# Summing keys and values over eight neighbours: three additions of halves in place of one strided tensor_reduce

## The chip, the cores and the metric

The kernel runs on one core of a Trainium2 chip. A core has five engines with instruction queues of their own, each executed in order: TensorE (PE in the profile; its weight loads are shown apart, as PEld), VectorE (DVE), ScalarE (ACT), GpSimd (POOL) and SyncE (SP), which here issues DMAs. They share the on-chip memory SBUF; TensorE writes its results to a second one, PSUM. Semaphores make an instruction on one engine wait for instructions on another. The metric is the time of one execution on the device, in microseconds (us); less is better.

## The reference

Attention with pooled keys and values, and behind it a layer of a transformer's feed-forward network:

```python
def _attn_ref(q, k, v):                       # 8 batches, 8 heads, 576 positions, 64 wide
    k_p = k.reshape(B, H, Sp, 8, D).mean(axis=3)      # 72 pooled keys: means of 8 neighbours
    v_p = v.reshape(B, H, Sp, 8, D).mean(axis=3)
    scores = scale * np.matmul(q, k_p.transpose(0, 1, 3, 2))
    ...                                       # softmax over the 72 keys
    return np.matmul(attn, v_p)
def _moe_ref(x, w_in, w_out):                 # 4608 tokens, 512 -> 2048 -> 512
    h = x @ w_in
    g = h * (1.0 / (1.0 + np.exp(-1.702 * h)))
    return g @ w_out
```

What the change touches is the sum over eight neighbours in the first two lines of the attention.

## The kernel before

The kernel works through the eight batches one after the other, and interleaves the attention of one batch with the feed-forward products of the batch before it, so that TensorE always has matmuls of one of the two. The order of all work on all engines is written out by hand in one long table (`ORDER`, a string of names such as `V:red1_0#0`, with V for VectorE, G for GpSimd, A for ScalarE, P for TensorE and D for a DMA); the program's code only says what each named task consists of and which buffers it reads and writes. So an engine never chooses: if the next task of its queue has to wait, all that stands behind it on that engine waits too.

For each batch b and each group u of four heads, keys and values of the first 512 positions are loaded into one SBUF tile `kv` (128 partitions, 2 x 512 numbers of fp32 in each). A partition holds, for each of two head pairs, eight neighbours of 64 numbers one behind the other. `spread` sums the eight neighbours into `red` (128 x 128), and then writes `red` into the block-diagonal tiles `kbd` (keys) or `vbd` (values) that TensorE multiplies with (a TENSOR_TENSOR on line 918). There are 32 such sums, four in each batch. Three of batch 0 are done by TensorE (line 886). The other 29 are done by VectorE with one `tensor_reduce` each: line 893 for five of batches 0 and 1 (named in `SUMMED`), where `red` is a PSUM buffer, and line 908 for the 24 of batches 2 to 7, where `red` lies in SBUF. The eight neighbours stand 64 numbers apart, so the reduce reads its 1024 numbers with a stride of 256 bytes.

The `kv` tile has a single buffer: the load of the next keys or values (SyncE, lines 797 and 811) waits until the sum has read the last ones. The PSUM buffers of `red` in batch 1 come from the same ring of two as those of the scores (`sps`, line 1126) and of attention times values (`pav`, lines 1365 to 1376).

Other names that are spoken of below: `stage` (lines 1762, 1790) and `xt`, `xs` (line 1457) are sums of weights and of inputs on VectorE or GpSimd, which the feed-forward products need; `ha` and `hb` (line 1880) are those products in PSUM; `shared` (line 1902) is VectorE's addition of an `hb`, which frees it for TensorE; `glall` (line 1934) and `gl` (line 1705) are differences that GpSimd or VectorE forms from two SBUF tiles; `w` and `raw` (lines 1641, 1627) are GpSimd's share in splitting the weights; `x` (line 1416) is VectorE's addition from a `pav`, which frees it; `vt` (line 1067) is a copy from SBUF to SBUF; `sc` and `tail` (lines 1198, 1232) belong to the softmax.

Of the kernel before, what the change touches and what calls it, by code (L numbers as in the profile page):

```python
# [14 lines left out]
ALU = mybir.AluOpType  # L15
AX = mybir.AxisListType
# [3 lines left out]
POOL = 8  # L20
# [553 lines left out]
def attention_moe_kernel(ctx: ExitStack, tc: tile.TileContext, q, k, v, w_in, w_out, out):  # L574


    nc = tc.nc
    B, H, S, D = q.shape
# [45 lines left out]
    def buf(pool, shape, dtype, tag, name, bufs=None, fifo=False):  # L624
        n = bufs or {"xpool": 2, "moe": 2, "ps_o": 4, "ps_h": 2, "ps_a": 2}.get(pool.name, 1)
        ring = rings.setdefault((pool.name, tag), Ring(n, fifo, pool.name))
        kw = {"bufs": bufs} if bufs else {}
        return Buf(ring, lambda: pool.tile(shape, dtype, tag=tag, name=name, **kw), name)
# [15 lines left out]
    def dve(n, emit, reads, writes, rate=1.0, due=None, also=(), port=False):  # L644
        return plan.add("DVE", 0.07 + n / 960.0 * rate, emit, reads, writes, due, also=also, port=port)
# [6 lines left out]
    def pe(ns, emit, reads, writes, due=None, also=(), mode="f32"):  # L652
        return plan.add("PE", ns * 1e-3, emit, reads, writes, due, also=also, mode=mode)
# [7 lines left out]
        out=mask4[0:96], in_=ident[0:96].rearrange("p (r h e) -> p h r e", r=4, h=4), axis=AX.XY, op=ALU.add  # L661
# [3 lines left out]
        out=mask4[96:128, 0:2],  # L665
        in_=ident[96:128].rearrange("p (r a e) -> p a r e", r=8, a=2),
        axis=AX.XY,
        op=ALU.add,
# [6 lines left out]
        out=mask, in_=ident.rearrange("p (r h e) -> p h r e", r=4, h=4), axis=AX.XY, op=ALU.add  # L675
# [3 lines left out]
        out=member, in_=ident.rearrange("p (r g e) -> p g r e", r=2, g=POOL), axis=AX.XY, op=ALU.add  # L679
# [92 lines left out]
    class Part:  # L772
# [8 lines left out]
        @property  # L781
        def ref(self):
            return (self.of, self.key)
# [91 lines left out]

    def spread(b, raw, bd, u, nm):

        if b < TURNED:
            red = buf(ps_h if b == 0 else ps_a, [P, 512], F32, "h" if b == 0 else "a", f"red{b}_{nm}")

            def summed():
                return red()[:, 0 : NP * D].rearrange("p (i d) -> p i d", i=NP)

            def windows():
                for w in range(POOL):
                    nc.tensor.matmul(
                        summed(), lhsT=ident, rhs=raw()[:, :, w * D : (w + 1) * D], start=w == 0, stop=w == POOL - 1
                    )

            if (b, nm) in SUMMED:  # L890
                dve(
                    1024,
                    lambda: nc.vector.tensor_reduce(
                        out=summed(), in_=raw().rearrange("p i (w d) -> p i d w", w=POOL), axis=AX.X, op=ALU.add
                    ),
                    [ref(raw)],
                    [red],
                    rate=1.75,
                    also=[bd],
                )  # L900
            else:
                pe(2 * POOL * 111, windows, [ref(raw)], [red], also=[bd])
        else:
            red = buf(att, [P, NP, D], F32, "red", f"red{b}_{nm}")
            summed = red
            dve(
                1024,
                lambda: nc.vector.tensor_reduce(
                    out=red(), in_=raw().rearrange("p i (w d) -> p i d w", w=POOL), axis=AX.X, op=ALU.add
                ),  # L910
                [ref(raw)],
                [red],
                rate=1.75,
                also=[bd],
            )
        dve(
            256,
            lambda: nc.vector.tensor_tensor(
                out=bd()[:, NP * u : NP * (u + 1)],
                in0=summed().unsqueeze(2).broadcast_to([P, NP, 2, D]),  # L920
                in1=mask2i.unsqueeze(1).unsqueeze(3).broadcast_to([P, NP, 2, D]),
                op=ALU.mult,
            ),
            [red],
            [(bd, u)],
            port=b >= TURNED,
        )
# [4 lines left out]
    def sum_keys(b, m):  # L932
# [6 lines left out]
        for u in range(NU):  # L939
            raw = m.k[u] if m.k else fetch_main(b, u, k)  # L940
            if b >= TURNED:
                tl = fetch_tail(b, u)
            spread(b, raw, m.kbd, u, f"k{u}")
            if b < TURNED and u == 0:
                tps = buf(ps_o if b == 0 else ps_a, [P, 512], F32, "o" if b == 0 else "a", f"tps{b}")
# [98 lines left out]
    def sum_values(b, m):  # L1044
        m.vbd = buf(att, [P, NJ, 2, D], F32, "bd", f"vbd{b}", fifo=True)
        for u in range(NU):
            raw = m.v[u] if m.v else fetch_main(b, u, v)
            spread(b, raw, m.vbd, u, f"v{u}")
# [1488 lines left out]
```

## Time and profile before

| | |
|---|---|
| time, median of 3 runs | 877.8 us (876.97, 877.8, 877.99) |
| span of the profiled execution, first to last instruction | 876.5 us |
| TensorE busy | 867.8 us, 99% |
| VectorE busy | 712.3 us, 81% |
| ScalarE busy | 529.5 us, 60% |
| GpSimd busy | 318.0 us, 36% |
| VectorE's reduces of lines 893 and 908 | 29 of some 2.0 us each |
| granted TensorE clock, mean | 1.00 |

The profiled execution is not one of the three timed runs; its span is 1.3 us under their median, and what lies before the first and after the last instruction is not in it. A page of the profile gives for each group of instructions its busy time and the idle time of its engine just before it with what ended it. The timeline gives single instructions with their start and length; one that waits inside the engine is simply longer than its like.

### The profile page before, as it was taken

The numbers are of one execution on the slowest core, as the hardware profiler recorded it, in microseconds if no ns is written. First come the engines' busy times: TensorE is split into PE (matmuls) and PEld (weight loads), VectorE is DVE, ScalarE is ACT, GpSimd is POOL, SyncE is SP. The second block draws the span as 40 slices with busy tenths as digits, with TensorE's granted clock in tenths as the row PEclk, the third lists the DMA queues.
The fourth block names the chain that finished last, engine by engine and source line by source line (L and its number), as shares of the span: only waits on it lengthen the run. The fifth ranks groups of instructions, "written<-read, shape, count | busy, mean of one in ns | idle before, by whom it ended". The sixth has DMA issues, their size and how long they took to land.

```text
span 876.5 us, 15636 instructions
## 1 busy us (share of the span) xinstructions
PE 867.8 (99%) x5322; PEld 775.8 (89%) x5322; DVE 712.3 (81%) x1413; ACT 529.5 (60%) x1170; POOL 318.0 (36%) x325
## 2 busy tenths in 40 slices
PE   8999999999999999999999999999999999999998
PEld 7889888888898999998999999999999988889998
DVE  6999988897879896788887877788878866778887
ACT  4987855547565774767566755677476743455430
POOL 2778753554321113222522242324522123432321
PEclk9999999999999999999999999999999999999999
DMA  9966444576577666756785777667766457978003
GB/s 275 377 219 185 131 133 162 167 228 199 173 226 218 213 209 211 232 159 209 239 245 160 219 215 231 191 200 213 213 200 194 155 182 217 332 230 298 1 13 85
DMA packets 146351, 174.31 MB, mean 199 GB/s; under 512 B 85216, under 2 KB 97504, under 8 KB 146272
## 3 DMA queue, kind: packets, MB, share of 16 engines
q1 hardware_dynamic: 141808, 165.32, 61.1%
q10 hardware_dynamic: 4464, 8.00, 2.5%
q8 instruction: 42, 0.69, 0.3%
q14 instruction: 37, 0.30, 0.1%
HBM read 141.95 MB, written 31.33 MB: 198 GB/s over the span
## 4 chain that ended last, share of the span: by engine, by line
PE 92%; SPq 2%; DVE 2%; DMA 2%; ACT 1%; issue 0%; POOL 0%; POOLq 0%; DVEq 0%; ACTq 0%
PE ha L1880 13%; PE hb L1880 10%; PE m L2386 9%; PE o L2086 8%; PE o L2087 8%; PE o L2088 8%; PE la L2155 5%; PE sps L1126 4%; PE h L1677 3%; PE h L1675 3%; PE h L1676 3%; PE o L1717 3%; PE o L1718 3%; PE o L1719 3%; PE lc L2155 2%; PE lb L2155 1%
## 5 line engine op out<-in xcount | busy, mean ns | idle before, releaser
L1934 POOL TENSOR_TENSOR glall<-shared,ghall 128x256 fp32r<-128x256 f32 x78 | 61.6, 795 | 200.2 <-ACT shared L1927 137.7
L2086 PE MATMUL o<-w,ghall 128*128 128x512 f32 x320 | 127.1, 397 | 0.0
L2087 PE MATMUL o<-w,ghall 128*128 128x512 f32 x320 | 126.2, 394 | 0.0
L2088 PE MATMUL o<-w,glall 128*128 128x512 f32 x320 | 124.9, 390 | 0.0
L2088 PEld LDWEIGHTS o<-w,glall 128*128 128x128 f32 x320 | 60.1, 188 | 13.8 <-DVE glall L1934 0.2
L1880 PE MATMUL ha<-xs,ws 128*128 128x256 f32 x480 | 70.9, 283 | 0.0
L1934 POOL TENSOR_TENSOR glall<-gall,ghall 128x256 fp32r<-128x256 f32 x43 | 33.4, 782 | 102.4 <-ACT gall L1927 73.1
L1880 PEld LDWEIGHTS ha<-xs,ws 128*128 128x128 f32 x480 | 66.2, 190 | 4.4 <-ACT gall L1895 0.2
L1880 PE MATMUL hb<-x,ws 128*128 128x256 f32 x480 | 67.1, 283 | 0.0
L2086 PEld LDWEIGHTS o<-w,ghall 128*128 128x128 f32 x320 | 60.6, 189 | 6.4
L2087 PEld LDWEIGHTS o<-w,ghall 128*128 128x128 f32 x320 | 60.6, 190 | 5.8
L1880 PEld LDWEIGHTS hb<-x,ws 128*128 128x128 f32 x480 | 63.3, 190 | 2.4
L1919 ACT ACTIVATE ghall<-shared 128x256 fp32r<-128x256 f32 x108 | 43.8, 416 | 34.8 <-DVE shared L1902 15.7
L1675 PE MATMUL h<-x,w 128*128 128x512 f32 (+1 forms) x160 | 57.5, 359 | 0.0
L1705 POOL TENSOR_TENSOR gl<-g,gh 128x512 fp32r<-128x512 f32 x27 | 36.6, 1354 | 57.3 <-ACT gh L1697 49.0
L1676 PE MATMUL h<-x,w 128*128 128x512 f32 (+1 forms) x160 | 55.5, 347 | 0.0
L1677 PE MATMUL h<-x,w 128*128 128x512 f32 (+1 forms) x160 | 55.5, 347 | 0.0
L1241 ACT COPY main<-sc 32x256 f32<-32x256 f32 (+2 forms) x109 | 48.6, 446 | 4.9 <-DVE sc L1198 2.5
L1902 DVE TENSOR_TENSOR shared<-shared,hb 128x256 f32<-128x256 f32 x81 | 33.4, 413 | 22.2 <-PE hb L1880 18.5
L1895 ACT COPY shared<-ha 128x256 f32<-128x256 f32 x63 | 23.3, 369 | 42.4 <-PE ha L1880 42.1
L1126 PE MATMUL sps<-k,qt 128*128 128x144 f32 x320 | 45.9, 287 | 0.0
L1717 PE MATMUL o<-w,gh 128*128 128x512 f32 x112 | 45.4, 405 | 0.0
(270 smaller groups left out, 2430.6 us busy)
## 6 DMA issues: line engine op xcount, KB each, us to landing
ws<-wd SPq DMA_DIRECT2D x144, 512.0 KB
shared<-wd SPq DMA_DIRECT2D x48, 256.0 KB
wd<-stage SPq DMA_DIRECT2D x16, 512.0 KB
raw<-in_moe_w_in_dram SPq DMA_DIRECT2D x15, 512.0 KB
raw<-in_moe_w_out_dram SPq DMA_DIRECT2D x15, 512.0 KB
kv_False<-in_k_dram SPq DMA_DIRECT2D x28, 256.0 KB
kv_True<-in_v_dram SPq DMA_DIRECT2D x28, 256.0 KB
out_dram<-osb ACTq DMA_DIRECT2D x28, 256.0 KB
```

What stands on the lines that cost most here:

```text
L1126: nc.tensor.matmul(ps()[:, t * PW : (t + 1) * PW], lhsT=qt()[:, s0 : s0 + P], rhs=m.k2()[:, jj], start=True, stop=True,)
L1675: nc.tensor.matmul(o, lhsT=w[:, 0, j], rhs=xs[:, 0], start=j == 0, stop=False)
L1676: nc.tensor.matmul(o, lhsT=w[:, 1, j], rhs=xs[:, 0], start=False, stop=False)
L1677: nc.tensor.matmul(o, lhsT=w[:, 0, j], rhs=xs[:, 1], start=False, stop=j == NJ - 1)
L1717: nc.tensor.matmul(o, lhsT=gh()[:, i, tok], rhs=w[:, 0], start=f == 0, stop=False)
L1880: nc.tensor.matmul(o, lhsT=wv()[:, r, jj], rhs=xo(k, jj), start=start and n == 0, stop=n == len(terms) - 1,  skip_group_check=not start,)
L1934: engine.tensor_tensor(out=gl(), in0=part(i), in1=gh().bitcast(F32), op=ALU.subtract)
L2086: nc.tensor.matmul(o(), lhsT=gh()[:, tok], rhs=w()[:, 0], start=start, stop=False)
L2087: nc.tensor.matmul(o(), lhsT=gh()[:, tok], rhs=w()[:, 1], start=False, stop=False)
L2088: nc.tensor.matmul(o(), lhsT=gl()[:, tok], rhs=w()[:, 0], start=False, stop=stop)
L2155: nc.tensor.matmul(bank(), lhsT=wv()[:, r, jj], rhs=xs[jj]()[:, k], start=start and n == 0, stop=n == len(terms) - 1, skip_group_check=not ...
L2386: nc.tensor.matmul(banks[i]()[:, i], lhsT=av(r)[:, i * P : (i + 1) * P], rhs=tv(k), start=p == 0 and n == 0 and (i == 0 or banks[0] is not ...
```

## The change

Each of VectorE's 29 reduces becomes three additions. The first adds the upper four neighbours to the lower four (2 x 256 numbers in each partition), in place in the `kv` tile. The second adds the upper two of these to the lower two (2 x 128), in place again. The third adds the last two and writes `red` (2 x 64). Each reads what the one before it wrote. Both inputs of each are in SBUF. The task has the same name, the same place in the order and the same dependences for the rest of the program; the order of the instructions on TensorE, ScalarE, GpSimd and SyncE is the same as before, and on VectorE three instructions stand wherever one stood.

```diff
     def spread(b, raw, bd, u, nm):
 
+        def tree(out):
+            r = raw()
+            for n in (4 * D, 2 * D, D):
+                to = r[:, :, 0:n] if n > D else out()
+                nc.vector.tensor_tensor(out=to, in0=r[:, :, 0:n], in1=r[:, :, n : 2 * n], op=ALU.add)
+
         if b < TURNED:
...
                 dve(
                     1024,
-                    lambda: nc.vector.tensor_reduce(
-                        out=summed(), in_=raw().rearrange("p i (w d) -> p i d w", w=POOL), axis=AX.X, op=ALU.add
-                    ),
+                    lambda: tree(summed),
...
             dve(
                 1024,
-                lambda: nc.vector.tensor_reduce(
-                    out=red(), in_=raw().rearrange("p i (w d) -> p i d w", w=POOL), axis=AX.X, op=ALU.add
-                ),
+                lambda: tree(red),
```

## Rows read from the trace of the kernel before

**Rows 1.** The page: the span, and busy time, share and instructions of each engine
```profile
span 876.5 us, 15636 instructions
PE 867.8 (99%) x5322; PEld 775.8 (89%) x5322; DVE 712.3 (81%) x1413; ACT 529.5 (60%) x1170; POOL 318.0 (36%) x325
```

**Rows 2.** TensorE's longest wait behind VectorE: us in total, times, longest us
```profile
PE pav L1365 <- DVE xt L1425: 0.7, 1, 0.7
```

**Rows 3.** Line 908, the reduces of keys: ns least/median/most, first and last start us
```profile
L908 DVE TENSOR_REDUCE red_k<-kv_False x12: 1928/2016/2072, 115.6 to 609.7; 128x128 f32<-128x1024 f32 x12
```

**Rows 4.** VectorE's additions and multiplications of 512, 256 and 128, from their lines
```profile
L1457 DVE TENSOR_TENSOR xt<-xt x3: 679/681/685, 236.0 to 424.8; 128x512 f32<-128x512 f32 x3
L2332 DVE TENSOR_TENSOR ou<-store x25: 408/419/427, 787.5 to 858.0; 128x256 f32<-128x256 f32 x25
L1198 DVE TENSOR_TENSOR tail<-sc,sps x2: 280/314/347, 24.2 to 44.2; 128x128 f32<-128x128 f32 x1, 128x192 f32<-128x192 f32 x1
```

**Rows 5.** Timeline at 527.5, VectorE and GpSimd: start us, length us, engine, line
```profile
527.53 0.87 DVE L1070 TENSOR_TENSOR vt<-tbd,vt 32x512 fp32r<-32x512 f32 x1
527.82 1.19 POOL L1934 TENSOR_TENSOR glall<-shared,ghall 128x256 fp32r<-128x256 f32 x1
528.43 0.85 DVE L918 TENSOR_TENSOR kbd<-red_k,mask2i 128x256 f32<-128x256 f32 x1
```

**Rows 6.** Timeline at 807.7, GpSimd behind four instructions of VectorE, the last shown
```profile
807.65 2.64 POOL L2332 TENSOR_TENSOR ou<-store 128x256 f32<-128x256 f32 x1 [10.21 <-DVE oc L2326]
...
809.01 0.69 DVE L2326 TENSOR_TENSOR oc<-ou,oc 128x512 fp32r<-128x512 f32 x1
```

**Rows 7.** Timeline at 80.1 to 84.4, values of batch 1
```profile
80.12 1.33 POOL L1641 TENSOR_TENSOR w<-raw,w 128x512 fp32r<-128x512 f32 x1 [0.48 <-ACT w L1634]
...
80.30 2.10 DVE L893 TENSOR_REDUCE red_v<-kv_True 128x128 f32<-128x1024 f32 x1 [0.45 <-DMA kv_True<-in_v_dram]
...
81.41 1.30 POOL L1705 TENSOR_TENSOR gl<-g,gh 128x512 fp32r<-128x512 f32 x1
...
82.67 1.04 POOL L1627 TENSOR_TENSOR raw<-raw 128x512 uint32<-128x512 uint32 x1
...
83.09 0.42 DVE L918 TENSOR_TENSOR vbd<-red_v,mask2i 128x256 f32<-128x256 f32 x1
...
84.39 0.65 PE L1126 MATMUL sps<-k,qt 128*128 128x144 f32 x4
```

**Rows 8.** Timeline at 130.6 to 139.1, keys of batch 2
```profile
130.56 0.76 POOL L1641 TENSOR_TENSOR w<-raws,w 128x256 fp32r<-128x256 f32 x1
130.57 2.02 DVE L908 TENSOR_REDUCE red_k<-kv_False 128x128 f32<-128x1024 f32 x1
...
131.26 3.08 POOL L1762 TENSOR_TENSOR stage<-w 128x512 f32<-128x512 f32 x2
...
138.24 0.42 DVE L1416 TENSOR_TENSOR x<-pav,x 128x256 fp32r<-128x256 f32 x1
...
139.06 0.39 PE L1365 MATMUL pav<-ah,vh 128*128 128x320 f32 x1
```

**Rows 9.** Timeline at 426.0 to 430.2, keys of batch 5
```profile
426.01 1.48 POOL L1457 TENSOR_TENSOR xt<-xt,xt 128x512 f32<-128x512 f32 x1
...
426.37 2.06 DVE L908 TENSOR_REDUCE red_k<-kv_False 128x128 f32<-128x1024 f32 x1
427.45 0.74 POOL L1934 TENSOR_TENSOR glall<-shared,ghall 128x256 fp32r<-128x256 f32 x1
...
428.16 1.29 POOL L1457 TENSOR_TENSOR xs<-xt,xs 128x512 fp32r<-128x512 f32 x1
428.35 1.38 DVE L1067 CAST vt<-tbd 96x512 fp32r<-96x512 f32 x1
...
429.65 0.40 DVE L1902 TENSOR_TENSOR shared<-shared,hb 128x256 f32<-128x256 f32 x1
...
430.24 0.64 PE L1880 MATMUL hb<-x,ws 128*128 128x256 f32 x4
```

## The prediction

> **What bounds the kernel now.** I read the page first: TensorE is busy for 867.8 of 876.5 us [rows 1], so all other engines together can be charged with no more than 8.7 us of its idle time. I then read the list of its waits. Behind VectorE there is one wait to speak of there, a single one of 0.7 us [rows 2]. VectorE is busy for 712.3 us [rows 1], and its reduces take 2.02 us each in the middle [rows 3], 58 us for the 29. A reader should see that these 58 us are almost wholly beside TensorE's work: making VectorE faster takes little off the end, since TensorE has next to nothing left to wait for. The reverse doesn't hold. A result of VectorE that comes too late stops TensorE at once, and a TensorE that is always busy can't make the stop good later. So the question is not only whether three additions are shorter than a reduce, but whether any of the 29 ends later, and by more than TensorE's reserve at that place.
>
> **The change part by part.** Removed: 29 x 2.02 = 58.6 us of VectorE [rows 3]. Added: 29 times an addition of 512, one of 256 and one of 128 numbers per partition. With nothing in the way these take 0.68, 0.42 and 0.28 us [rows 4], and a dependent instruction starts some 0.03 us after the one before it (528.43 against 527.53 + 0.87, [rows 5]): 1.44 us. So alone the tree is 0.58 us shorter, 16.8 us over the 29.
>
> The Trainium skill speaks against even this: "VectorE: DVE Perf Modes", section "The perf-mode tier table (the rule you actually need)", has tensor_reduce and fp32 tensor_tensor both at one element a cycle. By it an estimate for the reduce is 1024 / 0.96 GHz and a fixed part, some 1.2 us, and the tree would be the longer one by about 0.2 us. The measured reduce of 2.02 us disagrees with that page, and the measurement decides.
>
> What the reduce doesn't do, and the additions do, is to compete with GpSimd. The reduces stay between 1.93 and 2.07 us [rows 3], though GpSimd works in most of them. Instructions of VectorE with two inputs in SBUF are different. At 528.43 a `kbd` of 256 numbers takes 0.85 us in place of 0.42, and GpSimd's `glall`, itself held back by `vt`, ends at 529.01 [rows 5]. Three things are read from this. VectorE's instruction is held until about 0.13 us before GpSimd's ends (529.28 - 0.42 = 528.86, against 529.01). GpSimd's is held while VectorE's runs (1.19 us, against 0.74 for its like in [rows 9]). And a gap of 0.03 us between two instructions of VectorE is enough for a waiting GpSimd to go in between. A tree has two such gaps, so with GpSimd busy it can be held three times: before each addition, by up to one instruction of GpSimd, 0.74 to 1.30 us [rows 7, 9].
>
> The skill's "SBUF — State Buffer", section "SBUF: two separate sides", states the same as a rule: the port pair that the two engines share goes whole to whichever starts first, for its entire instruction, against an instruction of VectorE with two SBUF inputs. By that rule too the reduce, with one input, is free of it, and the tree is not; the rows agree.
>
> Where GpSimd rests, the tree ends 0.58 us earlier, and that is worth nothing but at the wait of 0.7 us [rows 2]: 0 to 0.7 us. I take 0, since a gain there needs a tree shortly before it that nothing else on VectorE waits behind, and keep 0.7 as the bound. Where GpSimd is busy I follow the rows, GpSimd's instructions in their order, with the rule above. Of the 29 places I price the three where the delay is largest beside the reserve. TensorE's reserve is the time from the end of the VectorE instruction that releases its matmul to that matmul's start.
>
> At 80.30 [rows 7], the values of batch 1: `w` runs on GpSimd since 80.12 and ends at 81.45, so the first addition begins at about 81.32 and ends at 82.00. `gl` goes in between and ends at 83.17; the second addition runs from 83.04 to 83.46; `raw` goes next, to 84.4, and the third ends at some 84.6, where the reduce ended at 82.40. That is 2.2 us late. Behind it in VectorE's queue stand two instructions on weights and `vbd`, which frees the PSUM buffer that the scores at 84.39 are written to. `vbd` ended at 83.51, a reserve of 0.88. TensorE loses 2.2 - 0.9 = 1.3 us. If the tree starts before `w`, which needs only 0.2 us (the reduce had itself waited 0.45 for its load), the first addition and not `w` goes first, and by the same steps the tree ends about 0.9 late: no loss.
>
> At 130.57 [rows 8], keys of batch 2: `w` of 0.76 started 0.01 us earlier. First addition 131.19 to 131.87; the first `stage`, of about 1.3 like `gl` [rows 7], to 133.05; second addition to 133.34; the second `stage` to 134.5; third addition to 134.7, where the reduce ended at 132.59: 2.1 late. VectorE is then busy without a break worth the name up to `x`, which ends at 138.66 and frees a `pav` for TensorE at 139.06: reserve 0.4, and 0.2 more for short gaps on the way. Loss 1.5. With the tree ahead of `w` by a hundredth, it is 0.9 late, and the loss 0.3.
>
> At 426.37 [rows 9], keys of batch 5: `xt` runs until 427.49. First addition 427.36 to 428.04; `glall` to 428.65; second addition to 428.94; `xs` to 430.1; third addition to 430.25, where the reduce ended at 428.43: 1.8 late. `vt` behind it was itself held by `xs`, some 1.0 of its 1.38 us, so it ends 430.7 at best, and 1.3 later if the next `xt` goes ahead of it. `shared`, which ended at 430.05, ends 1.0 to 2.0 later; it frees the `hb` that TensorE starts at 430.24, reserve 0.2. Loss 0.8 to 1.8; I take 1.4, the middle being 1.3 and the later order the one that the rule gives more often.
>
> Sum: 1.3 + 1.5 + 1.4 = 4.2 us. I take it for the whole, since the errors on its two sides are alike: with the lucky order in the first two places it falls to 0 + 0.3 + 0.8 = 1.1; and there are four more places where GpSimd is busy and the reserve is under the delay, each worth 0.2 to 0.6 by the same steps, which I leave as the upper side, some 1.5 more. The gain of 0.7 at most stands against that. GpSimd loses up to 0.7 us at each held instruction, but it is busy for only 36% [rows 1] and mostly ahead of its readers; I cost this at nothing, and at 1 to 3 us if that reserve fails. SyncE's next load of `kv` waits for the third addition in place of the reduce; the one load that was late at all is the one at 80.30.
>
> **The rivals.** *VectorE keeps its turn between the three additions*, and GpSimd waits for all of them. For it: at 807.65 a GpSimd addition of 0.74 takes 2.64 us, while additions of VectorE go past it, the last of which runs from 809.01 to 809.70 [rows 6]. Against it: those follow each other without a gap and don't read one another's results, where the steps of a tree do, and a dependent start leaves a gap. Then a tree is held once only: at 80.30 it ends 0.4 late, at 130.57 not at all (131.19 + 1.44 = 132.63), at 426.37 0.4 late with 0.2 of reserve. The loss is 0.2, the gain 0 to 0.7: 877.6 us, not slower. This decides if the gap between dependent additions is no longer an opening for GpSimd.
>
> *The delays spread*: all seven places lose, GpSimd's own delays reach TensorE through `glall` and `stage`, and late trees meet new work of GpSimd. Price: 4.2 + 0.3 for the worse order at 426, + 1.5 for the four places, + 2 for GpSimd: 8 us, 885.8. For it speaks that VectorE is 81% busy [rows 1], so delays take long to be worked off; against it that GpSimd is idle for 64%.
>
> *Faster*: 16.8 us less of VectorE reach the end after all. TensorE's idle time behind VectorE, 0.7 us [rows 2], caps that at 877.1, which is no measurable difference; more than that needs a mechanism that I don't see in the rows, such as matmuls slowed unseen by VectorE's reads.
>
> **How the numbers follow.** The profiled execution spans 876.5 us, 1.3 us under the median of 877.8 shown; the loss is added to the median: 877.8 + 4.2 = 882.0. Chances: the forecast 0.54 (878.9 to 884.5), delays that spread 0.14 (885.8), VectorE keeps its turn or the orders fall luckily 0.27 (877.6), faster 0.05. The range reaches from a little under the case that is not slower to the one that spreads, 877.2 to 886.0. A measurement of this kernel can tell some 0.2%, 1.76 us, from no change: below 876.0 is faster, above 879.6 slower. Faster 0.05; same 0.27; slower 0.68 (the little of the forecast that lies under 879.6 is set against the upper end of the lucky orders).
>
> **What would show it.** On VectorE the 29 reduces are replaced by 87 additions of least lengths 0.68, 0.42 and 0.28 us; where GpSimd is at work, by longer ones, whose excess is GpSimd's remainder less 0.13. VectorE's busy time should fall by far less than 17 us, and may rise. GpSimd's `glall`, `gl` and `stage` near trees are longer. TensorE's list of waits has new entries behind VectorE at 84, 139 and 430 us (scores behind `vbd`, `pav` behind `x`, `hb` behind `shared`), of 1 to 2 us each, and its idle time grows by as much as the time does. The prediction is wrong if the additions show no excess under GpSimd, if GpSimd never gets in between two additions of a tree, or if trees end late and TensorE still doesn't wait.

## The result, and the profile after

| | before | after |
|---|---|---|
| time, median of 4 runs | 877.54 us (876.97 to 877.99) | 889.24 us (889.11 to 889.67) |
| ratio, with its 95% interval | | 1.0131 (1.0117 to 1.0146) |
| span of the profiled execution | 876.5 us | 887.3 us |
| forecast | | 882.0 us, range 877.2 to 886.0 |

The kernel became slower by 11.7 us. The sign was forecast, the size was not: the loss is 2.8 times the 4.2 us of the sum, and the time lies above the range. The page of the profile after, in the form of [rows 1], with its chain of work that ended last:

```profile
span 887.3 us, 15690 instructions
...
PE 872.1 (98%) x5322; PEld 776.6 (88%) x5322; DVE 716.4 (81%) x1471; ACT 529.0 (60%) x1170; POOL 326.0 (37%) x325
...
PE 82%; DVE 6%; DMA 5%; SPq 3%; ACT 2%; issue 2%; POOL 0%; DVEq 0%; ACTq 0%
```

TensorE's share of the chain was 92% before. VectorE has 58 instructions more (two for each of 29 places) and is busy for 4.1 us more, not 16.8 less. GpSimd does the same 325 instructions in 8.0 us more. TensorE's idle time, the span less its busy time, grew from 8.7 to 15.2 us; its busy time grew by 4.3 us with the same number of matmuls. The list of TensorE's waits (us in total, times, longest) names where; [rows 2] was the only entry behind VectorE of that size in the running part of the kernel before, and it is still there, unchanged:

```profile
PE tpt L1272 <- DVE tail L1200: 4.0, 1, 4.0
PE hb L1882 <- DVE shared L1904: 1.9, 2, 1.6
...
PE pav L1367 <- DVE xt L1427: 0.7, 1, 0.7
PE pav L1367 <- DVE x L1418: 0.5, 1, 0.5
...
PE pav L1369 <- DVE at L1316: 0.3, 1, 0.3
PE o L2090 <- POOL glall L1936: 0.3, 1, 0.3
```

A wait in this list isn't the whole loss, since matmuls behind a wait can be slower too. Both traces hold the same 5322 matmuls in the same order, so each can be set against itself: how much later does it start after than before, counted from the first instruction of the span? This lateness of TensorE grows in few places:

| stretch of the trace before, us | lateness at its start and end | grown by | the tree ahead of it, in the trace after |
|---|---|---|---|
| 0 to 40 | 0.00, -0.60 | -0.6 | |
| 90 to 110 | -0.56, 5.00 | 5.6 | at 90.98 (91.13 before), values of batch 1 |
| 110 to 145 | 5.00, 7.05 | 2.0 | at 135.80 (130.57 before), keys of batch 2 |
| 260 to 280 | 7.05, 7.37 | 0.3 | at 269.1 |
| 425 to 440 | 7.32, 9.20 | 1.9 | at 433.57 (426.37 before), keys of batch 5 |
| 600 to 625 | 9.29, 10.87 | 1.6 | at 618.99 (609.70 before), keys of batch 7 |
| all others | | 0.0 | |

Past 40 us that is 11.4 us, close to the 11.7 of the medians; the first 40 us, with the first loads, happened to be 0.6 shorter in the trace after. The expectations below name the large steps by another measure, the start-to-start excess (the distance of two successive matmul starts less the shortest that such two have elsewhere), and with it by 5.5, 1.8, 1.7 and 1.7 us.

The additions are on line 882 of the kernel after, and its other lines stand 2 to 6 further down than before. By form (busy time of the group, mean ns of one, idle time before), in place of the reduces of [rows 3]:

```profile
L882 DVE TENSOR_TENSOR kv_False<-kv_False 128x512 f32<-128x512 f32 x14 | 13.0, 928 | 0.0
...
L882 DVE TENSOR_TENSOR kv_False<-kv_False 128x256 f32<-128x256 f32 x14 | 10.4, 746 | 0.5
...
L882 DVE TENSOR_TENSOR red_k<-kv_False 128x128 f32<-128x128 f32 x14 | 9.6, 684 | 0.5
...
L882 DVE TENSOR_TENSOR red_v<-kv_True 128x128 f32<-128x128 f32 x14 | 7.1, 504 | 0.5
```

The second additions of keys and values together take 20.4 us, the first 24.7, the third 16.7: 61.8 us for 28 trees, 2.2 us for one; with nothing in the way it would be 1.4. The smallest additions show the hold best: 128 numbers take 0.50 and 0.68 us in the mean, where [rows 4] has 0.28 for that size. The whole excess goes with GpSimd. Of the 87 additions 51 start while it runs nothing, and none of them is over 0.02 us longer than 0.68, 0.42 or 0.29 us. The other 36 start under an instruction of GpSimd, and each is longer by what was left of that, less 0.13 us, to within 0.06.

**The hole of 4.0 us.** This is the kernel before at this place, a stretch that the rows ahead of the prediction don't show (start, length, engine, line):

```profile
96.96 0.16 DVE L1192 TENSOR_SCALAR sm<-sm 128x16 f32<-128x16 f32 x1
...
98.05 0.29 DVE L1198 TENSOR_TENSOR tail<-sc,sm 128x128 f32<-128x128 f32 x1
...
98.63 0.39 PE L1719 MATMUL o<-w,gl 128*128 128x512 f32 x1
...
98.86 0.38 PE L1270 MATMUL tpt<-ident,tail 128*64 128x128 f32 x2
98.90 1.30 POOL L1705 TENSOR_TENSOR gl<-g,gh 128x512 fp32r<-128x512 f32 x1 [4.10 <-ACT gh L1697]
```

And this the kernel after; the first row of VectorE is the first addition of the tree:

```profile
90.94 1.30 POOL L1707 TENSOR_TENSOR gl<-g,gh 128x512 fp32r<-128x512 f32 x1 [0.51 <-ACT gh L1699]
...
90.98 1.81 DVE L882 TENSOR_TENSOR kv_True<-kv_True 128x512 f32<-128x512 f32 x1
...
92.19 2.68 POOL L1629 TENSOR_TENSOR raw<-raw 128x512 uint32<-128x512 uint32 x2
...
92.82 1.15 DVE L882 TENSOR_TENSOR kv_True<-kv_True 128x256 f32<-128x256 f32 x1
...
94.01 1.02 DVE L882 TENSOR_TENSOR red_v<-kv_True 128x128 f32<-128x128 f32 x1
...
98.07 0.39 PE L1721 MATMUL o<-w,gl 128*128 128x512 f32 x1
...
98.34 1.66 POOL L1707 TENSOR_TENSOR gl<-g,gh 128x512 fp32r<-128x512 f32 x1 [3.46 <-ACT gh L1699]
...
98.79 1.24 DVE L1194 TENSOR_SCALAR sm<-sm 128x16 f32<-128x16 f32 x1
...
100.52 1.74 POOL L1643 TENSOR_TENSOR w<-raw,w 128x512 fp32r<-128x512 f32 x1
...
101.03 1.37 DVE L1200 TENSOR_TENSOR tail<-sc,sm 128x128 f32<-128x128 f32 x1
...
102.46 0.64 PE L1272 MATMUL tpt<-ident,tail 128*64 128x128 f32 x2 [4.00 <-DVE tail L1200]
```

Read it in three steps. First, the tree is held before each of its additions, by `gl` and twice by a `raw`, and takes 4.05 us where the reduce took 2.06. Second, `sm` and `tail` are two of the shortest instructions of VectorE. Before, they ended ahead of GpSimd's `gl`, `tail` by only 0.56 us. Now they come after it has started, and are held by `gl` and by `w`: 1.24 in place of 0.16 us, 1.37 in place of 0.29. Third, TensorE's clock. The windows of the same trace (us, busy time of PE, PEld, DVE, ACT and POOL, the granted clock, DMA share and GB/s) show the granted clock at half, 1.2 of 2.4 GHz, behind the 4.0 us in which TensorE did nothing, and the matmul rows show it too: 0.63 in place of 0.39 us.

```profile
101.00:102.00 1.00, 0.00 (x0) 0.00 (x0) 1.00 (x2) 0.00 (x0) 1.00 (x1) 1.00 0.76 244
103.00:104.00 1.00, 1.00 (x4) 0.81 (x4) 1.00 (x4) 0.83 (x3) 0.00 (x0) 0.50 0.22 41
```

```profile
103.75 0.63 PE L1679 MATMUL h<-x,w 128*128 128x512 f32 x1
```

To put numbers to the steps I set the two traces against each other by the last matmul ahead of the wait, 98.63 before and 98.07 after: the trace after runs 0.56 us early there. On that scale the tree starts 0.41 us late (left over from earlier trees) and `red_v` is ready 95.03 + 0.56 - 93.19 = 2.40 us late. The reserve was 98.86 - 98.34 = 0.52, so the tree alone should cost 1.9 us. GpSimd's `gl` and `w` add 1.08 and 1.08 us more at `sm` and `tail`, together 2.2. The slow matmuls add 1.4 (TensorE's lateness is 3.60 at the waiting matmul and 5.00 at 110). The sum is 5.4, against 5.6 in the table.

**The place that went by the prediction.** At 433.57, the answer to [rows 9]:

```profile
433.33 1.47 POOL L1459 TENSOR_TENSOR xt<-xt,xt 128x512 f32<-128x512 f32 x1
...
433.57 1.78 DVE L882 TENSOR_TENSOR kv_False<-kv_False 128x512 f32<-128x512 f32 x1
...
434.77 1.18 POOL L1936 TENSOR_TENSOR glall<-shared,ghall 128x256 fp32r<-128x256 f32 x1
...
436.27 1.27 DVE L882 TENSOR_TENSOR red_k<-kv_False 128x128 f32<-128x128 f32 x1
...
439.33 0.86 PE L1882 MATMUL hb<-x,ws 128*128 128x256 f32 x5 [1.61 <-DVE shared L1904]
```

The working had the tree end 3.88 us after its start; it ended after 3.97. It had TensorE lose 1.4 us of a possible 0.8 to 1.8; it waits for 1.61, and the step in the table is 1.9.

### The profile page after: what moved, and what is told of

Read it like the earlier page. It is cut to its first block, busy times and chain, and to the rows that moved or that the text cites. A ratio compares the mean times of both kernels' runs of the same rounds, so it can differ in the third digit from the quotient of the medians.

```text
span 887.3 us, 15690 instructions
## 1 busy us (share of the span) xinstructions
PE 872.1 (98%) x5322; PEld 776.6 (88%) x5322; DVE 716.4 (81%) x1471; ACT 529.0 (60%) x1170; POOL 326.0 (37%) x325
## 4 chain that ended last, share of the span: by engine, by line
PE 82%; DVE 6%; DMA 5%; SPq 3%; ACT 2%; issue 2%; POOL 0%; DVEq 0%; ACTq 0%
PE ha L1882 12%; PE hb L1882 9%; PE m L2388 9%; PE o L2088 8%; PE o L2089 8%; PE o L2090 8%; PE la L2157 5%; PE sps L1128 4%; DMA raw<-in_moe_w_out_dram 3%; PE lc L2157 2%; PE h L1677 2%; PE h L1679 2%; PE h L1678 2%; PE o L1719 2%; PE o L1721 2%; PE o L1720 2%
```

## The experiments

Two theories were held against each other. **A**: GpSimd holds the additions, VectorE is late, and the lateness puts VectorE's later instructions under GpSimd's next work, so a place can cost far more than its own delay less the reserve. **B**: each place costs its own delay less its reserve, as the prediction summed it. Rivals that leave GpSimd out (**C**: three dependent instructions, or writing into `kv`, cost time at every place) were kept beside them. Each time stands against the kernel before in the same series. The first 40 us differ between executions by chance: at 40 us TensorE is 0.7 us ahead of the trace before in that of `two_trees` and 0.9 behind it in that of `late_trees`, and these three kernels are the same up to 115 us. So from a single trace only steps behind 40 us are read.

**Early and late places.** The tree in one part of the places, the old reduce in the rest:

```diff
+        def strided(out):
+            nc.vector.tensor_reduce(
+                out=out(), in_=raw().rearrange("p i (w d) -> p i d w", w=POOL), axis=AX.X, op=ALU.add
+            )
+
+        total = tree if b < TURNED else strided
...
-                    lambda: tree(summed),
+                    lambda: total(summed),
```

The early places are those of batches 0 and 1, as here; for the late ones the condition is `b >= TURNED`.

> Additions in the first two batches only (5 of 29 places, 6.8 to 91 us), the strided reduce in the other 24. Theory A (a tree that GpSimd holds makes VectorE late, and the lateness brings VectorE's later instructions under GpSimd's next work, so a place costs more than its own delay less the reserve): the hole of 4.0 us at 102 us and the slow matmuls behind it stay as in the changed kernel, and the time is 877.5 + 5.5 = 883.0 us (882 to 884). Rival B (each place costs its own delay less the reserve, as the prediction summed it): at most the 1.3 us of 80 us and 0.6 of 91 us, 877.5 to 879.4 us, and the loss lies in the later batches. Rival C (the loss has nothing to do with the places): a share of 5/29 of 11.7, 879.5 us.

884.39 us, ratio 1.0076 (1.0061 to 1.0091), 6.6 us more than before from five trees, 0.4 us above the range that A gave. The hole is there, one wait of 4.0 us behind `tail`.

> Additions in batches 2 to 7 only (24 of 29 places), the strided reduce in the first two batches. Theory A: the holes at 141, 275, 439 and 625 us stay, TensorE's start-to-start excess there being 1.8 + 0.2 + 1.7 + 1.7 = 5.4 us in the changed kernel: 877.5 + 5.4 = 882.9 us; the early hole at 102 us is absent. As GpSimd's and VectorE's work meets in other phases after another early part, single holes may move: 881 to 885. Rival B: 1.5 + 1.4 of the two places priced, 880.4 us. Rival C: 24/29 of 11.7, 887.2 us.

882.02 us, ratio 1.0055 (1.0036 to 1.0074), 4.2 us. TensorE waits at the same late places as with all trees, `hb` behind `shared` for 1.6 us once and `pav` behind `x` for 0.5. But the trace is of the longest of the four runs, 885.02 us; the other three took 881.27 to 882.15, so one of its waits may be missing in them. The two parts together make 10.8 of the 11.7 us. The split is near the one that A read from the trace, and C (2.0 us early, 9.7 late) falls.

**One tree alone**, the one ahead of the hole:

```diff
+        total = tree if (b, nm) == (1, "v1") else strided
```

> Additions at one place only, the values of batch 1 that VectorE sums at 91 us; the strided reduce at the 28 others. Theory A: this one tree makes the whole early hole: red_v is ready some 1.8 us late, VectorE's short instructions on sm and tail at 97 to 102 us then fall under GpSimd's gl and w (1.2 and 1.4 us in place of 0.16 and 0.29), TensorE waits about 4 us for tail and runs at the half clock for some 3 us after it: 877.5 + 5.5 = 883.0 us. Rival B: lateness of 1.8 less what the short gaps of VectorE take back and a reserve of 0.5: 878.0 to 878.9 us. If the hole needs the lateness that earlier trees leave, there is no loss here: 877.5.

879.42 us, ratio 1.0029 (1.0014 to 1.0044): 1.6 us, neither the 5.5 of A nor the 0.5 to 1.4 of B. The trace says why:

```profile
98.48 1.47 POOL L1714 TENSOR_TENSOR gl<-g,gh 128x512 fp32r<-128x512 f32 x1 [3.70 <-ACT gh L1706]
98.75 1.36 DVE L1207 TENSOR_TENSOR tail<-sc,sm 128x128 f32<-128x128 f32 x1
...
100.16 0.41 PE L1279 MATMUL tpt<-ident,tail 128*64 128x128 f32 x2 [1.55 <-DVE tail L1207]
```

Without the earlier trees this one starts 0.37 us ahead of `gl`, where with them it starts 0.04 behind it. So it is held twice and not three times, and `red_v` is 1.1 us late instead of 2.4. `sm` then still passes ahead of `gl`, and only `tail` is held. My expectation was wrong in taking the state that the earlier trees leave as unimportant: 0.4 us of it go with a wait of 4.0 in place of 1.55. Two of the ten runs took 883.09 and 884.44 us, at a mean granted clock of 0.997 and 0.996 where the others have 0.999 or 1.00. That is what A expected, and the long hole may have come about in them by chance; no trace of them was kept, so it isn't shown.

**Lateness without any addition.** The kernel before, with the reduce done twice at this place:

```diff
+        def strided(times):
+            for _ in range(times):
+                nc.vector.tensor_reduce(
...
+                    lambda: strided(2 if (b, nm) == (1, "v1") else 1),
```

> The kernel before, with the strided reduce done twice at one place, the values of batch 1 at 91 us (the second writes the same sums again): red_v is ready 2.0 us later there, and no addition is in the kernel. Theory A (lateness alone is enough: the instructions on sm, main and tail behind it meet GpSimd's gl and w): tail grows from 2.0 late to about 4, TensorE waits 3 to 4 us for it near 102 us and runs at the half clock after it: 881 to 883 us. Rival B (only the delay less the reserve of some 0.5 us): a wait of 1.5 us, 879 us.

884.17 us, ratio 1.0066 (1.0050 to 1.0083), 6.1 us more:

```profile
98.86 1.67 POOL L1709 TENSOR_TENSOR gl<-g,gh 128x512 fp32r<-128x512 f32 x1 [4.10 <-ACT gh L1701]
...
99.32 1.24 DVE L1196 TENSOR_SCALAR sm<-sm 128x16 f32<-128x16 f32 x1
...
101.57 1.37 DVE L1202 TENSOR_TENSOR tail<-sc,sm 128x128 f32<-128x128 f32 x1
...
103.00 0.42 PE L1274 MATMUL tpt<-ident,tail 128*64 128x128 f32 x1 [4.02 <-DVE tail L1202]
```

No tree is in this kernel, and the hole is the same to 0.02 us, with the half clock behind it; the slow matmuls cost 2.6 us here, which brings the time over the 881 to 883 us that A expected. B is out: 2.4 us of lateness with a reserve of 0.5 don't cost 1.9 but 6.

**The size of the hole, with GpSimd out of the way.** All 29 trees; the `gl` at 98 us and the `w` at 100.5 us become plain copies on ScalarE. The first lines of the edit (the one for `w` is alike):

```diff
         def upper():
             nc.scalar.activation(out=gh(), in_=h(), func=AF.Gelu_apprx_sigmoid)
+            if now:
+                nc.scalar.copy(out=gl(), in_=g())
...
         def rest(engine):
-            engine.tensor_tensor(out=gl(), in0=g(), in1=gh().bitcast(F32), op=ALU.subtract)
+            if not now:
+                engine.tensor_tensor(out=gl(), in0=g(), in1=gh().bitcast(F32), op=ALU.subtract)
```

> The changed kernel with all 29 trees; two instructions of GpSimd, the gl that starts at 98 us and the w that starts at 100.5 us, are replaced by plain copies of the same 512 numbers on ScalarE, ahead of the time at which GpSimd would run them (left out: the two subtractions, so gl and w hold the unsplit numbers there). Theory A (the size of the hole at 102 us is set by these instructions of GpSimd, VectorE's lateness only starts it): sm takes 0.16 and tail 0.29 us again, tail ends some 1.7 us after TensorE is ready in place of 4.0, the granted clock doesn't fall: 2.3 + 1.35 = 3.6 us less than the changed kernel, 885.6 us (884.5 to 886.5). Rival B (the hole is VectorE's own lateness): a hole of 4.0 us as before, 889 us.

884.42 us, ratio 1.0074 (1.0059 to 1.0089), 4.8 us under the changed kernel where 3.6 was expected. By the starts of the matmuls the step at this place goes from 5.6 to 2.0 us, 3.6 as expected; the other 1.2 us aren't assigned. VectorE is as late as before at the tree, `sm` and `tail` have their old lengths, and the granted clock stays at 1.00:

```profile
98.72 0.16 DVE L1194 TENSOR_SCALAR sm<-sm 128x16 f32<-128x16 f32 x1
...
99.82 0.28 DVE L1200 TENSOR_TENSOR tail<-sc,sm 128x128 f32<-128x128 f32 x1
...
100.16 0.41 PE L1272 MATMUL tpt<-ident,tail 128*64 128x128 f32 x2 [1.76 <-DVE tail L1200]
```

> The same replacement of the two instructions of GpSimd (the subtractions left out) in the kernel before, with the strided reduce: the control. There VectorE's instructions on sm and tail end before GpSimd's gl starts, so nothing should be gained: 877 to 878.5 us by every theory; a gain of over 1.8 us would say that moving the two helps by itself.

878.14 us, ratio 1.0001 (0.9991 to 1.0010). Taking the two instructions off GpSimd gives nothing where VectorE is in time. So they make the difference between a hole of 1.76 and one of 4.00 us, and do so only once VectorE is late. The lateness of `red_v` and the hole, side by side (lateness worked out as above, by the last matmul ahead of the wait):

| kernel | `red_v` late by, us | TensorE waits, us | granted clock behind it |
|---|---|---|---|
| before | 0 | 0 | 1.00 |
| one tree | 1.1 | 1.55 | 1.00 |
| one addition and a reduce (below) | 1.3 | 1.74 | 1.00 |
| reduce twice | 2.4 | 4.02 | 0.50 |
| all trees | 2.4 | 4.00 | 0.50 |
| all trees, `gl` and `w` off GpSimd | 2.4 | 1.76 | 1.00 |

**All trees but four.** The reduce is kept at the four places ahead of the four largest steps of the table:

```diff
+        total = tree if (b, nm) not in {(1, "v1"), (2, "k1"), (5, "k1"), (7, "k1")} else strided
```

> Additions at 25 of the 29 places; the strided reduce at the four whose trees lie ahead of the waits of the changed kernel: values of batch 1 (91 us in that kernel), and the second keys of batches 2, 5 and 7 (136, 434 and 619 us). Theory A (the whole loss hangs on these four): 877.5 + 0.2 (the wait at 275) + up to 0.5 for the place at 80 us = 877.5 to 878.5 us, and TensorE's list of waits has no entry behind VectorE over 0.7 us. Rival C (each tree costs a little, 11.7 / 29): 887.6 us. Rival D (late trees elsewhere fill the gap when these four go): 880 to 884 us.

878.77 us, ratio 1.0008 (0.9999 to 1.0018), with 25 trees. Of TensorE's waits behind VectorE past 60 us two are left, that of [rows 2] and a small one behind `gall`:

```profile
PE pav L1374 <- DVE xt L1434: 0.7, 1, 0.7
PE hb L1889 <- DVE gall L1911: 0.4, 1, 0.4
```

Without four trees of the 29, 0.7 of the 11.7 us are left, so the loss hangs on these four. That they alone would make it isn't shown, as the one at 91 us cost 1.6 us by itself and 5.6 behind the earlier ones. VectorE is busy for 708.9 us here, 3.4 less than before, and nothing is gained by it.

**Two places that the prediction priced**, 130.57 and 426.37, alone (the additions where `(b, nm)` is `(2, "k1")` or `(5, "k1")`):

> Additions at two places only, the second keys of batches 2 and 5 (130.57 and 426.37 us in the kernel before), the strided reduce at the 27 others. The prediction's terms for the two: 1.5 + 1.4 = 2.9 us, 880.4 to 880.7 us. By TensorE's start-to-start excess in the changed kernel: 1.8 + 1.7 = 3.5 us, 881.0 to 881.3 us. If the holes there need the lateness that other trees leave: 878 to 879.

881.02 us, ratio 1.0040 (1.0026 to 1.0054): 3.1 us, where the prediction's two terms make 2.9; the time falls in the second of the three ranges. By the starts of the matmuls TensorE loses 1.5 us at the first place and 1.9 at the second. At the first, `w` starts 0.02 us ahead of the tree (129.79 against 129.81), which is the order that the prediction priced. The waits:

```profile
PE hb L1889 <- DVE shared L1911: 1.6, 1, 1.6
...
PE pav L1376 <- DVE at L1323: 0.3, 1, 0.3
PE pav L1374 <- DVE x L1425: 0.3, 1, 0.3
```

**One hold in place of three.** One addition, then a strided reduce over what is left:

```diff
-            for n in (4 * D, 2 * D, D):
-                to = r[:, :, 0:n] if n > D else out()
-                nc.vector.tensor_tensor(out=to, in0=r[:, :, 0:n], in1=r[:, :, n : 2 * n], op=ALU.add)
+            n = 4 * D
+            nc.vector.tensor_tensor(out=r[:, :, 0:n], in0=r[:, :, 0:n], in1=r[:, :, n : 2 * n], op=ALU.add)
+            nc.vector.tensor_reduce(
+                out=out(), in_=r[:, :, 0:n].rearrange("p i (w d) -> p i d w", w=4), axis=AX.X, op=ALU.add
+            )
```

> At all 29 places one addition of 512 numbers, then one strided tensor_reduce over the four sums that are left: about 0.68 + 0.03 + 1.07 = 1.8 us alone, against 1.44 for three additions and 2.02 for the reduce. Theory A: only the first instruction can be held by GpSimd, and once, by 1.3 us at most; the reduce behind it isn't held. A place ends at most 1.8 + 1.2 - 2.0 = 1.0 us late in place of 1.8 to 2, most of that inside the reserves: 877.5 to 880 us, no wait of 4 us at 102, a wait of at most 1 us at 440. Rival C (additions that write back into kv, dependent instructions, whatever GpSimd does): half of the loss or more, 883 us and up.

879.20 us, ratio 1.0015 (1.0006 to 1.0024). The addition is held as in the tree (those of keys take 952 ns in the mean), the reduce behind it is not: 1.09 us for 512 numbers, as expected. The trace is of the longest of the ten runs, 880.72 us. In it the wait at `tail` is 1.7 us, the one at `hb` near 433 us is 0.15.

```profile
L882 DVE TENSOR_REDUCE red_k<-kv_False 128x128 f32<-128x512 f32 x14 | 15.2, 1089 | 0.5
```

A dependent second instruction and a write into `kv` are in this kernel too, at all 29 places, and it loses 1.1 us in all; so they are not what costs 11.7.

**Another form of addition**, in the hope that GpSimd lets it pass:

```diff
-                nc.vector.tensor_tensor(out=to, in0=r[:, :, 0:n], in1=r[:, :, n : 2 * n], op=ALU.add)
+                nc.vector.scalar_tensor_tensor(
+                    out=to, in0=r[:, :, 0:n], scalar=1.0, in1=r[:, :, n : 2 * n], op0=ALU.mult, op1=ALU.add
+                )
```

> All 29 trees as in the changed kernel, with each addition written as scalar_tensor_tensor, (in0 * 1.0) + in1, in place of tensor_tensor: the same sizes, the same buffers, the same waits and order. In the trace of the kernel before, the scalar_tensor_tensor on 32-bit integers with two SBUF inputs stays at 0.63 to 0.69 us while GpSimd works. Theory A: if the fp32 form is let through likewise, the trees take 0.68 + 0.42 + 0.28 us everywhere, no hole appears and the time is that of the kernel before, 876.8 to 877.9 us. If the fp32 form is held like tensor_tensor, the additions show the same excess and the time is 889 us. Rival C (three dependent instructions, their semaphores or their writes into kv cost the time, not GpSimd): 887 to 889 us with additions of unchanged lengths.

888.96 us, ratio 1.0128 (1.0113 to 1.0143), and the additions are held as before (ns least, median, most; first and last start):

```profile
L882 DVE SCALAR_TENSOR_TENSOR kv_False<-kv_False x28: 425/706/1781, 61.5 to 620.2; 128x512 f32<-128x512 f32 x14, 128x256 f32<-128x256 f32 x14
...
```

The hope failed: the form of the instruction is no way out. As a time the run doesn't set A apart from C, since with the hold in place both give this one. Its trace does at one place, the second keys of batch 7. There the tree meets GpSimd otherwise by chance: the third addition takes 0.29 us (at 621.78) in place of 1.43, the `kbd` behind it 0.43, the tree 2.59 in place of 3.57, and TensorE loses nothing where it lost 1.6 with all trees. The same three additions, held for 1 us less, cost nothing. No kernel of the study beats the one before.

## Why the prediction was right in its sign and wrong in its size

- **What bounds the kernel**: right. 25 trees that take 3.4 us off VectorE bring nothing, and the late ones stop TensorE at once. The wait of 0.7 us behind `xt` is still 0.7, so the gain taken as 0 was 0.
- **The cost of a tree**: right. Least lengths are 0.63, 0.42 and 0.29 us; 15 of the 29 trees take 2.19 us or more, up to 4.05, as they are held up to three times (the rows at 90.98). The 0.13 us by which a hold ends early is what the 36 held additions show; the text's own figures for it, 528.86 against 529.01, make 0.15. VectorE's busy time rose, which the text had as a possibility. GpSimd got in between dependent additions, so the rival in which VectorE keeps its turn is out.
- **The place at 80.30** (1.3 us): the loss was 0. There the tree started ahead of `w` (79.12 against 79.48), the order for which the text had the tree 0.9 us late and no loss. It took 3.41 us and was 0.8 late by TensorE's matmuls; the scores that were to wait for `vbd` didn't, but some 0.4 us of lateness went on to the next tree. In the trace of `early_trees` the scores do wait for `vbd`, and 0.4 us is lost.
- **The place at 426.37** (1.4 us): right in mechanism and size. The tree met `xt`, `glall` and `xs` as the text had it, `vt` was held behind the next `xt`, the later order, and `shared` came too late: 1.9 us in the changed kernel and in a kernel of two trees.
- **The place at 130.57** (1.5 us): the size, 2.0, was met by luck. The tree starts ahead of `w` there, the order for which the text had it 0.9 us late and a loss of 0.3. It was 1.1 late. The rest comes from behind it: a `stage` of VectorE, 0.68 us before, falls under GpSimd's and takes 1.78.

```profile
135.80 1.86 DVE L882 TENSOR_TENSOR kv_False<-kv_False 128x512 f32<-128x512 f32 x2
136.20 1.19 POOL L1643 TENSOR_TENSOR w<-raws,w 128x256 fp32r<-128x256 f32 x1
...
138.90 1.78 DVE L1764 TENSOR_TENSOR stage<-w 128x512 f32<-128x512 f32 x1
```

The wait came behind another `x` than the one named, the first behind the tree (133.15 in the kernel before, 140.60 after), with a reserve of 1.55 us that the working had not looked at, and behind `at` next to it. Only in the kernel of two trees did the priced order come about, and there the loss was 1.5. With the orders of the changed kernel the text's three terms make 0 + 0.3 + 1.4 = 1.7 us, where 0, 2.0 and 1.9 were measured.
- **The step that failed** is the price itself, a tree's own delay less TensorE's reserve, and with it the choice "Of the 29 places I price the three where the delay is largest beside the reserve", with the rest on the upper side at "0.2 to 0.6" for four and nothing for the others. The place at 91.13, which the text doesn't list (the expectation for `early_trees` puts it at 0.6), cost 5.6 us. The place at 609.70 isn't priced either; it cost 1.6. By the starts of the matmuls past 40 us the error is 11.4 - 4.2 = 7.2 us, and this is it: 5.6 + 1.6, 0.3 at 269.1 and 1.0 by which the two places above were short, less the 1.3 of 80.30 that didn't come.
- **Why the place at 91 was so mis-sized**, in its three parts. Delays were worked out one place at a time, with the order of the trace before; 0.4 us from earlier trees turned that order, and one more hold followed (1.1 against 2.4 us late, by the run with one tree). The price was then delay less reserve; but after a delay the instructions behind the tree meet other work of GpSimd, and `sm` and `tail` were held where they had not been before (2.2 us; the run with `gl` and `w` on ScalarE takes it away, the one with the reduce done twice has it without a tree). And behind a wait of 4.0 us the clock was at half (1.4 us), which has no place in the sum. At 618.99 the second part can be read in the trace alone: behind a tree that took 3.57 us, a `kbd` at 622.60 takes 1.47 us in place of 0.42, under a new `xt` of GpSimd. No run tests that place by itself, but in the trace of `stt_trees`, where that `kbd` isn't held, nothing is lost there.

```profile
622.49 1.28 POOL L1459 TENSOR_TENSOR xt<-xt,xt 128x512 f32<-128x512 f32 x1
622.60 1.47 DVE L920 TENSOR_TENSOR kbd<-red_k,mask2i 128x256 f32<-128x256 f32 x1
```

- **The rival that the delays spread** named just this ("late trees meet new work of GpSimd"), with a chance of 0.14 and a price of 885.8 us. Its mechanism is what happened. Its price was made of the same small terms and a round 2 us, so even it fell 3.4 us short.
- **GpSimd's own delays at nothing**: nearly right; 0.3 us of waiting behind a `glall` at 627.82 is all that the list has. SyncE's loads: no new wait of TensorE behind a load of `kv` appears.

The rule of the Trainium skill that was used, "SBUF — State Buffer", section "SBUF: two separate sides", held for the tree in both forms of the addition, which have two inputs in SBUF, and for the reduces, which pass. It doesn't hold for the `scalar_tensor_tensor` on 32-bit integers below, which has two inputs in SBUF and passes; there the measurement decides. The same section also names instructions of VectorE in a 2-port mode. The `sm`, which has one input in SBUF and takes 1.24 us under `gl` and 0.16 without it, would fall under that; that it runs in such a mode, no run here shows. The prediction had used the rule for the tree alone, not for what stands behind it.

## What to carry to other kernels

Where VectorE and GpSimd hold each other, follow a delay past the first waiting matmul: list what GpSimd starts in the next 10 us, and which short instructions of VectorE now end just ahead of it, since each that falls under a GpSimd instruction adds to the price (1.1 us each for `sm`, `tail` and `stage` here). Give a reserve in two numbers, to the reader on TensorE and to the next start on GpSimd; the second was 0.56 us at `tail`, and the 2.2 us hung on it. The reduce that takes 1.9 to 2.1 us in every trace, whatever GpSimd does, was worth more to this full schedule than three additions that take 1.4 us when alone.

## What the runs showed of the hardware that was not expected

- The granted clock fell to half behind waits of 4.0 us (four kernels) and stayed at 1.00 behind waits of 1.55 to 1.76 us (three kernels). At half, a matmul of 512 columns started 0.20 us later behind the one before it than at the full clock; the slow stretch cost 1.4 to 2.6 us.
- The hole was 4.00 us in three kernels in which trees made VectorE late, and 4.02 us in the one in which a second reduce did, `red_v` being 2.4 us late in all four. 2.2 us of it are two instructions of GpSimd, whatever the cause of the lateness.
- An fp32 `scalar_tensor_tensor` with two inputs in SBUF is held (up to 1.78 us for what takes 0.68 alone). The one on 32-bit integers in the splitting of the weights isn't, though its inputs lie in SBUF too:

```profile
L1620 DVE SCALAR_TENSOR_TENSOR raw<-raw,e x30: 629/680/694, 10.9 to 108.9; 128x512 uint32<-128x512 uint32 x30
```

What sets the two apart, the type, the operation or the layout of the inputs, stays open. The `tensor_scalar` on 32-bit integers (line 1614) passes as well, 0.70 us at 89.43 under a `w` in the kernel before, where the fp32 `sm` is held; that points to the type and doesn't show it.
